# Holding one constants transfer behind the activation-table load, and moving a second norm tile to ScalarE, in a fused spectral-mixer kernel

## Chip, cores, metric

One core of a Trainium2 chip. The metric is device time in microseconds (us) of one execution.

## The reference, cut to what matters

```python
def reference(A_x, A_w_r, A_w_i, B_x, B_w1, B_b1, B_w2, B_b2):
    x = A_x                                               # (1, 2048, 512) bf16
    h = x + _A_ref(_layernorm(x, axis=-1), A_w_r, A_w_i)  # rfft2 -> times (w_r + i w_i) -> irfft2
    h2 = h + _B_ref(_layernorm(h, axis=-1), B_w1, B_b1, B_w2, B_b2)  # layernorm, MLP along the sequence, gelu
    return h2
```

The kernel does the transforms as matmuls with constant DFT matrices. Taking off a row's mean changes only the zero frequency along the row, which becomes zero and is left out of the transform, so the first stage needs only the row's reciprocal deviation, and that is multiplied into the DFT constants (not into x).

## The kernel before

x lies in 16 tiles of 128 rows x 512. For each tile: statistics of x, a reciprocal root (`rs`), the scaling of that tile's constants FP into FS (`fs`), then four matmuls of FS with x (`f1`), then an evacuation (`ys`), which copies the result out of TensorE's accumulators to Y. All of Y is needed before the second stage (`f2`). The order of this front is given by hand, engine by engine:

```python
STAT_ACT = (3,)                      # tiles whose statistics ScalarE makes; VectorE makes the others
FS_ENG = {0: "act", 3: "act", 7: "act", 9: "dve", 11: "dve", ...}   # who scales the constants; the rest GpSimd
FRONT = {
    "dve": """bn_0 ag_0 bn_1 ag_1 bn_2 bn_4 ag_2 bn_5 ag_4 bn_6 ag_5 bn_7 ag_6 bn_8 ag_7 bn_9 ag_8 ...
    "act": """rs_0 fs_0 rs_1 s1_3 s2_3 rs_2 rs_3 fs_3 rs_4 ys_0 rs_5 ys_1 ys_3 rs_6 ...
    "pool": """fs_1 bv_3 fs_2 fs_4 fs_5 fs_6 fs_8 fs_10 fs_12""",
    ...
}
WARM_AFTER = (3, 2, 0, 1, 1, 0, 0, 1, 0, 0, 0, 0, 0, 0, 0, 0)  # matmuls on zeros behind the n-th tile of f1
# ... (cut)
for q, (a, b) in enumerate(((0, 2), (2, 4), (4, 6), (6, 8), (8, 12))):
    ldx(a, b, 99 - q)                # x by tiles, SyncE's queue
ldf(2, 90)                           # constants piece 2 (tiles 8-11)
ldx(12, 16, 89)
ldf(3, 88)
ldf(0, 92, "act")                    # piece 0 (tiles 0-3), 256 KB, ScalarE's queue
ldf(1, 91, "act")                    # piece 1 (tiles 4-7), 256 KB, ScalarE's queue
act("table", T["tb"][:, 0:1], EPS[:, 0:1], ACT.Abs_reciprocal_sqrt, 1, ...)   # loads the table
# ... (cut)
def stat_act(i):                     # two passes over the tile on ScalarE, sums by accumulator
    act(f"s1_{i}", junk()[:, :], x, ACT.Identity, 512, ins=[x], accum=SM[:, i:i + 1], prio=25)
    act(f"s2_{i}", junk()[:, :], x, ACT.Square, 512, ins=[x], accum=V1[:, i:i + 1], prio=25)
    # ... bv_i on GpSimd, then rs_i on ScalarE, then fs_i
# bn_i / ag_i: bn_stats and bn_aggr of tile i on VectorE, then rs_i on ScalarE, then fs_i
```

Each engine runs its list strictly in order and waits on counters of the others: an instruction whose input is late holds up everything behind it in its list. The whole kernel:

## Time and profile before

| | before |
|---|---|
| time, median of 3 runs | 131.98 us (131.97 to 132.01) |
| span of the profiled run | 130.2 us |
| TensorE busy | 93% of the span |
| VectorE / ScalarE / GpSimd busy | 54% / 48% / 8% |
| second stage starts (end of the front) | 18.09 us |
| x 0-1, 2-3, 6-7, 8-11 landed | 4.64, 6.13, 7.38, 8.85 us |

A tile's landing is read as the issue's start plus its time to landing.

### The profile page before, as it was taken

What the parts mean: (1) busy time and instruction counts of PE and PEld (TensorE: products, weight loads), DVE (VectorE), ACT (ScalarE), POOL (GpSimd) and SP (SyncE); (2) the same over time, 40 slices, a digit from 0 to 9 for tenths busy, and PEclk for the clock granted to TensorE, in tenths of its full rate; (3) what the DMA queues carried; (4) which work ended last, traced back from release to release, by engine and by line L of the source; (5) the groups of instructions that cost most, each with busy time, mean ns of one, the idle gap of its engine ahead of it and who ended that gap; (6) DMA issues with size and microseconds to landing.
All of it is one profiled execution on the core that took longest, in us unless ns stands there. A gap on an engine that the chain in (4) does not pass through costs nothing.

```text
span 130.2 us, 1995 instructions
## 1 busy us (share of the span) xinstructions
PE 121.6 (93%) x763; PEld 73.6 (57%) x773; DVE 70.2 (54%) x130; ACT 62.8 (48%) x144; POOL 10.7 (8%) x30
## 2 busy tenths in 40 slices
PE   6799889999978989999999999999999999999990
PEld 2155656788766645544444444456666666666660
DVE  0599868999973999999981000000332422423322
ACT  4299975969866999957679622222000000000000
POOL 0089910000300000000000000000000000000000
PEclk9999999999999999999999999999999999999999
DMA  3999999999999999995000000000112112111121
GB/s 98 353 401 377 286 276 289 294 241 264 369 425 423 408 409 409 417 267 151 0 0 0 0 0 0 0 5 0 40 40 81 40 40 81 45 62 59 40 81 43
DMA packets 17337, 22.17 MB, mean 170 GB/s; under 512 B 2768, under 2 KB 13264, under 8 KB 17328
## 3 DMA queue, kind: packets, MB, share of 16 engines
q1 hardware_dynamic: 17040, 21.52, 49.1%
q10 hardware_dynamic: 288, 0.52, 1.2%
q8 instruction: 6, 0.10, 0.3%
q14 instruction: 3, 0.02, 0.1%
HBM read 19.95 MB, written 2.10 MB: 169 GB/s over the span
## 4 chain that ended last, share of the span: by engine, by line
PE 76%; ACT 12%; DVE 6%; DMA 3%; issue 2%
PE ps L556 75%; ACT Y L574 4%; DVE V L826 3%; DMA X<-in_A_x_dram 3%; ACT rs L574 2%; ACT JK L574 2%; ACT EO L574 2%; ACT FS L574 1%; DVE Y L743 1%; ACT PQ L574 1%; DVE OUT L931 1%; DVE st L681 1%; DVE FS L659 0%; PE ps L647 0%; ACT r L574 0%
## 5 line engine op out<-in xcount | busy, mean ns | idle before, releaser
L556 PE MATMUL ps<-HH,W 128*128 128x512 bf16 (+1 forms) x173 | 40.1, 380 | 0.4 <-DVE TT L894 0.2
L556 PE MATMUL ps<-GT,W 128*128 128x512 bf16 (+1 forms) x172 | 37.9, 379 | 0.2
L931 DVE SCALAR_TENSOR_TENSOR OUT<-ps,B2f,H 128x512 bf16<-128x512 f32 x16 | 12.0, 751 | 46.8 <-PE ps L556 46.8
L556 PEld LDWEIGHTS ps<-GT,W 128*128 128x128 bf16 (+1 forms) x176 | 25.5, 145 | 12.6
L556 PEld LDWEIGHTS ps<-HH,W 128*128 128x128 bf16 (+1 forms) x176 | 17.4, 100 | 19.4 <-issue 0.6
L826 DVE TENSOR_TENSOR V<-ps,W 128x2048 bf16<-128x2048 f32 (+1 forms) x8 | 15.8, 2020 | 0.3
L574 ACT ACTIVATE JK<-H,nm 128x512 bf16<-128x512 bf16 x16 | 11.6, 723 | 3.9 <-DVE H L901 3.7
L574 ACT ACTIVATE GT<-ps,B1f 128x512 bf16<-128x512 f32 (+1 forms) x11 | 7.0, 691 | 12.8 <-PE ps L556 12.7
L681 DVE BATCH_NORM_STATS2 st<-X 128x6 f32<-128x512 bf16 x15 | 9.8, 666 | 3.6 <-DMA X<-in_A_x_dram 3.6
L901 DVE TENSOR_TENSOR H<-ps,TT 128x512 bf16<-128x512 f32 x16 | 10.9, 683 | 0.1
L574 ACT ACTIVATE PQ<-ps 128x512 bf16<-128x512 f32 (+1 forms) x16 | 9.2, 588 | 3.6 <-PE ps L556 3.5
L556 PE MATMUL ps<-EM,V 128*128 128x128 bf16 x128 | 9.8, 220 | 0.4 <-ACT PQ L574 0.3
L556 PE MATMUL ps<-FS,X 128*128 128x256 bf16 x64 | 8.6, 274 | 1.1 <-ACT FS L574 0.5
L574 ACT ACTIVATE EO<-ps 128x512 bf16<-128x512 f32 x16 | 9.2, 594 | 0.9 <-PE ps L556 0.9
L574 ACT ACTIVATE CS<-ps 128x512 bf16<-128x512 f32 (+1 forms) x16 | 8.9, 588 | 1.2 <-PE ps L556 1.2
L556 PEld LDWEIGHTS ps<-EM,V 128*128 128x128 bf16 x128 | 7.9, 98 | 2.3 <-issue 1.1
L556 PE MATMUL ps<-EM,Y 128*128 128x256 bf16 x64 | 8.8, 273 | 0.4 <-DVE Y L743 0.4
L556 PE MATMUL ps<-EM,PQ 128*128 128x256 bf16 x64 | 8.6, 273 | 0.5 <-ACT PQ L574 0.5
L647 PE MATMUL ps<-ZT 128*128 128x512 bf16 x19 | 7.0, 487 | 2.3 <-DVE ZT L594 1.2
L574 ACT ACTIVATE Y<-ps 128x512 bf16<-128x512 f32 (+1 forms) x15 | 7.9, 566 | 0.2
L892 DVE TENSOR_TENSOR TT<-ps,X 128x256 f32<-128x256 f32 x16 | 6.7, 419 | 2.4 <-PE ps L556 2.4
L659 POOL TENSOR_SCALAR FS<-FP,rs 128x256 bf16<-128x256 bf16 x8 | 7.4, 938 | 6.6 <-ACT rs L574 6.4
(38 smaller groups left out, 76.9 us busy)
## 6 DMA issues: line engine op xcount, KB each, us to landing
W<-in_B_w_dram SPq DMA_DIRECT2D x8, 688.0 KB, 9.5
W<-in_B_w_dram SPq DMA_DIRECT2D x10, 512.0 KB, 16.3
out_dram<-OUT SPq DMA_DIRECT2D x16, 128.0 KB, 1.7
W<-in_A_w_r_dram SPq DMA_DIRECT2D x4, 257.0 KB, 4.5
W<-in_A_w_i_dram SPq DMA_DIRECT2D x4, 257.0 KB, 5.4
X<-in_A_x_dram SPq DMA_DIRECT2D x4, 256.0 KB, 5.1
X<-in_A_x_dram SPq DMA_DIRECT2D x2, 512.0 KB, 6.7
W<-in_A_w_r_dram SPq DMA_DIRECT2D x4, 192.8 KB, 3.5
```

Of the source, the lines that this page charges most:

```text
L556: return K.op(name, "pe", lambda eng, bank: eng.matmul(outf(bank), lhsT, rhs, start=start, stop=stop), ins=ins or [lhsT, rhs], occ=occ, la ...
L574: return eng.activation(dst, s, func, **kw)
L647: return K.op(name, "pe", lambda eng, bank: eng.matmul(ps[:, bank, :], ZT[:, 0:NP], ZT[:, :], start=True, stop=True), ins=[ZT[:, :]], occ= ...
L659: dve(f"fs_{i}", lambda eng, bank: eng.tensor_scalar(FS[:, i, :, :], FP[:, i, :, :], rs, None, op0=ALU.mult), [FP[:, i, :, :], rs], [FS[:, ...
L681: dve(f"bn_{i}", lambda eng, bank, i=i, x=x: eng.bn_stats(ST[:, i, 0:6], x), [x], [ST[:, i, 0:6]], 512, prio=25)
L743: dve(name, lambda eng, bank: eng.tensor_copy(dst, src(bank)), [], [dst], n, unit=unit, prio=28, last=last)
L826: return eng.tensor_tensor(vout, s, win, ALU.mult)
L892: dve(f"tl_{s2}", lambda eng, bank, tt=tt, xl=xl: eng.tensor_tensor(tt[:, 0, :], ps[:, bank, 256:512], xl, ALU.add), [xl], [tt[:, 0, :]], ...
L901: return eng.tensor_tensor(hs.rearrange("p (h d) -> p h d", h=2), e, tt[:, :, :], ALU.add)
L931: dve(f"fin{s2}", lambda eng, bank, dst=dst, bia=bia, hs=hs: eng.scalar_tensor_tensor(dst, ps[:, bank, :], bia, hs, op0=ALU.add, op1=ALU.add),
```

## The change

The intent: keep piece 1 of the constants, which only tile 4 and later need, out of the way of the first x tiles; use ScalarE's idle time before the first root for a second tile's statistics; adapt the order of the front to that. Core of the diff:

```diff
-STAT_ACT = (3,)
+STAT_ACT = (1, 3)
-FS_ENG = {0: "act", 3: "act", 7: "act", 9: "dve", ...}
+FS_ENG = {3: "act", 7: "act", 5: "dve", 9: "dve", ...}
 FRONT = {
-    "dve": """bn_0 ag_0 bn_1 ag_1 bn_2 bn_4 ag_2 bn_5 ag_4 bn_6 ag_5 bn_7 ag_6 bn_8 ag_7 bn_9 ag_8 ...
+    "dve": """bn_0 ag_0 bn_2 ag_2 bn_4 bn_5 ag_4 bn_6 ag_5 bn_7 ag_6 bn_8 ag_7 fs_5 bn_9 ag_8 ...
-    "act": """rs_0 fs_0 rs_1 s1_3 s2_3 rs_2 rs_3 fs_3 rs_4 ys_0 rs_5 ys_1 ys_3 rs_6 ...
+    "act": """s1_1 s2_1 rs_0 rs_1 rs_2 s1_3 s2_3 rs_4 rs_3 fs_3 ys_0 rs_5 ys_1 rs_6 ys_3 ...
-    "pool": """fs_1 bv_3 fs_2 fs_4 fs_5 fs_6 ...
+    "pool": """bv_1 fs_0 bv_3 fs_1 fs_2 fs_4 fs_6 ...
-N_GATED = 2
-WARM_AFTER = (3, 2, 0, 1, 1, 0, 0, 1, 0, 0, 0, 0, 0, 0, 0, 0)
+GATED = (("bn_0", 2), ("s2_1", 2))
+WARM_AFTER = (3, 0, 0, 0, 0, 1, 0, 0, 1, 0, 0, 0, 3, 0, 0, 0)
-LAST_WARM = 7
+LAST_WARM = 12
-    ldf(1, 91, "act")
-    act("table", ...)
+    table = act("table", ...)
+    ldf(1, 91, "act", after=[table])
```

The warm-ups (matmuls on zeros, meant to keep TensorE's clock from falling) are regrouped too: two more run early, and three now stand behind tile 12's matmuls (the rest of the diff is cut).

More of the change, by code (lines that the diff above doesn't have):

```diff
@@ L492, in memory_layout @@
     return L
-STAT_ACT = (3,)
-RS_GROUPS = ((0,), (1,), (2,), (4,), (5,), (6, 7), (8,), (9, 10), (11, 12), (13,), (14, 15))
-FS_ENG = {0: "act", 3: "act", 7: "act", 9: "dve", 11: "dve", 13: "dve", 14: "dve", 15: "dve"}
+STAT_ACT = (1, 3)
+RS_GROUPS = ((0,), (2,), (4,), (5,), (6, 7), (8,), (9, 10), (11, 12), (13,), (14, 15))
+FS_ENG = {3: "act", 7: "act", 5: "dve", 9: "dve", 11: "dve", 13: "dve", 14: "dve", 15: "dve"}
 Y_EVAC = (("single", ("act",), ("act",)),) * 6 + (("single", ("dve",), ("act",)), ("single", ("dve",), ("act", "act")))
 FRONT = {
-    "dve": """bn_0 ag_0 bn_1 ag_1 bn_2 bn_4 ag_2 bn_5 ag_4 bn_6 ag_5 bn_7 ag_6 bn_8 ag_7 bn_9 ag_8 bn_10 ag_9 bn_11 ag_10 bn_12 ag_11
+    "dve": """bn_0 ag_0 bn_2 ag_2 bn_4 bn_5 ag_4 bn_6 ag_5 bn_7 ag_6 bn_8 ag_7 fs_5 bn_9 ag_8 bn_10 ag_9 bn_11 ag_10 bn_12 ag_11
         fs_9 ag_12 bn_13 fs_11 ag_13 bn_14 bn_15 ag_14 ag_15 fs_13 fs_14 fs_15 ys_12 ys_14
         tl_0 th_0 h_0 tl_1 th_1 h_1 hh_0""",
-    "act": """rs_0 fs_0 rs_1 s1_3 s2_3 rs_2 rs_3 fs_3 rs_4 ys_0 rs_5 ys_1 ys_3 rs_6 ys_2 fs_7 rs_8 ys_4 ys_5 rs_9 ys_7 rs_11 ys_6 ys_8
-        rs_13 ys_9 ys_10 rs_14 ys_11 ys_13 yh_150 yh_151
+    "act": """s1_1 s2_1 rs_0 rs_1 rs_2 s1_3 s2_3 rs_4 rs_3 fs_3 ys_0 rs_5 ys_1 rs_6 ys_3 ys_2 rs_8 fs_7 ys_5 rs_9 ys_4 ys_6 rs_11 ys_7 ys_8
+        ys_9 rs_13 ys_10 rs_14 ys_11 ys_13 yh_150 yh_151
         eo_0 eo_1 eo_2 eo_3 eo_4 q_0 r2_0 eo_5""",
-    "pool": """fs_1 bv_3 fs_2 fs_4 fs_5 fs_6 fs_8 fs_10 fs_12""",
-    "pe": """f1_0 f1_1 f1_3 f1_2 f1_4 f1_5 f1_7 f1_6 f1_8 f1_9 f1_10 f1_11 f1_12 f1_13 f1_14 f1_15""",
+    "pool": """bv_1 fs_0 bv_3 fs_1 fs_2 fs_4 fs_6 fs_8 fs_10 fs_12""",
+    "pe": """f1_0 f1_1 f1_3 f1_2 f1_5 f1_4 f1_6 f1_7 f1_8 f1_9 f1_10 f1_11 f1_12 f1_13 f1_14 f1_15""",
 }
 N_WARM = 9
-N_GATED = 2
-WARM_AFTER = (3, 2, 0, 1, 1, 0, 0, 1, 0, 0, 0, 0, 0, 0, 0, 0)
+GATED = (("bn_0", 2), ("s2_1", 2))
+WARM_AFTER = (3, 0, 0, 0, 0, 1, 0, 0, 1, 0, 0, 0, 3, 0, 0, 0)
 V_SPLIT = (7,)
-LAST_WARM = 7
+LAST_WARM = 12
 MM1B_FROM = {5: 54000.0, 6: 62000.0}
@@ L600, in build_kernel @@
     ldf(0, 92, "act")
-    ldf(1, 91, "act")
-    act("table", T["tb"][:, 0:1], EPS[:, 0:1], ACT.Abs_reciprocal_sqrt, 1, ins=[EPS[:, 0:1]], prio=95)
+    table = act("table", T["tb"][:, 0:1], EPS[:, 0:1], ACT.Abs_reciprocal_sqrt, 1, ins=[EPS[:, 0:1]], prio=95)
+    ldf(1, 91, "act", after=[table])
     dma("ld_EMR", EM[:, 0:2048], cin["EMR"][:, :], 1 << 19, outs=[EM[:, 0:2048]], prio=44)
@@ L695, in build_kernel @@
             stat_dve(g)
-    bn0 = [o for o in K.ops if o.name == "bn_0"]
-    for w_ in range(N_GATED):
-        warm(f"warmb{w_}", wu, 50, after=bn0, occ=427.0)
+    for g_, n_ in GATED:
+        for w_ in range(n_):
+            warm(f"warm_{g_}_{w_}", wu, 50, after=[o for o in K.ops if o.name == g_], occ=427.0)
     f1u, lastmm = {}, {}
```

## The prediction

> **What bounds the kernel now.** I read four views in this order: the chain that ended last, the timeline of each engine in the first 20 us, the transfers of the first 5 us, and the timeline of VectorE between 18 and 40 us.
>
> The chain in order of time shows where an earlier front could pay.
>
> ```profile
> 0.72 3.92 DMA X<-in_A_x_dram
> 4.67 0.71 DVE st L681
> 5.39 0.20 DVE mv L682
> 5.61 0.30 ACT rs L574
> 5.94 0.51 ACT FS L574
> ...
> 6.70 1.23 ACT JK L574 x4
> ...
> 16.26 0.48 DVE FS L659 x2
> 16.74 1.21 DVE Y L743 x2
> 17.95 0.14 issue
> 18.09 13.40 PE ps L556 x163
> 31.48 0.02 issue
> 31.51 4.50 DVE V L826 x2
> ```
>
> Start, length, what. Nothing runs for 4.64 us but the arrival of the first two x tiles; then one statistics pair on VectorE, and from 5.61 to about 16.2 us ScalarE with hardly a break (the windows give it 5.00 busy in 10 to 15 us, 4.32 in 5 to 10). The second DFT stage starts at 18.09 us, when all of Y is evacuated. After 46 us the chain is matmuls to the end at 127 us, so what the front gains is handed on only if everything between 18 and 46 us moves too.
>
> The start of ScalarE's work, from its timeline (start, length, instruction, idle before):
>
> ```profile
> 5.61 0.29 ACT L574 ACTIVATE rs<-mv,eps 128x1 f32<-128x1 f32 x1 [3.01 <-DVE mv L682]
> 5.94 0.51 ACT L574 ACTIVATE FS<-FP,rs 128x256 bf16<-128x256 bf16 x1
> 6.41 0.29 ACT L574 ACTIVATE rs<-mv,eps 128x1 f32<-128x1 f32 x1
> 6.61 0.61 ACT L574 ACTIVATE JK<-X 128x512 bf16<-128x512 bf16 x1
> ```
>
> ScalarE idles 3.01 us before 5.61, 0.94 us of it with x already there. That is the hole which tile 1's statistics are to fill.
>
> The transfers in half-microsecond stretches (last three columns: granted clock, DMA share, GB/s):
>
> ```profile
> 2.00:2.50 0.50, 0.50 (x3) 0.22 (x2) 0.00 (x0) 0.49 (x2) 0.00 (x0) 1.00 0.46 147
> 2.50:3.00 0.50, 0.50 (x3) 0.23 (x2) 0.00 (x0) 0.10 (x1) 0.00 (x0) 1.00 0.87 270
> 3.00:3.50 0.50, 0.50 (x3) 0.16 (x2) 0.00 (x0) 0.00 (x0) 0.00 (x0) 1.00 0.81 287
> 3.50:4.00 0.50, 0.50 (x2) 0.15 (x1) 0.00 (x0) 0.00 (x0) 0.00 (x0) 1.00 0.95 324
> ```
>
> The engines are near saturation from 2.5 us. The landing times in the trace: constants piece 0 at 4.46 us, x 0-1 at 4.64, constants piece 1 at 5.66, x 2-3 at 6.13, x 4-5 at 6.77, x 6-7 at 7.38. The packet records by queue put some 160 KB of piece 1 in front of x's 4.64.
>
> VectorE from 18 us:
>
> ```profile
> 19.91 2.36 DVE L811 TENSOR_TENSOR V<-ps,W 128x1024 bf16<-128x1024 f32 x2 [0.76 <-PE ps L556]
> 22.41 15.98 DVE L826 TENSOR_TENSOR V<-ps,W 128x2048 bf16<-128x2048 f32 x8
> ```
>
> The filter products run back to back, about 2.28 us each, and end at 38.39. The fourth of the big ones starts at 29.16 us and is the first to need the last group of filter weights, whose final transfer (issued at 22.34, 6.3 us to landing) is down at 28.67. VectorE's wait for that passed at 28.71, so the weights have only about 0.45 us to spare.
>
> **What the Trainium skill says.** "DMA: Bandwidth & Descriptors", section "Issuing engines are not separate DMA queues": transfers issued by ScalarE and SyncE end up on the same 16 engines and interleave; its section "Queues, rings and completion order" says that each engine takes turns between queues packet by packet. The trace agrees: until 3.75 us the two queues move near-equal amounts, and x's 256 KB takes 3.92 us from issue to landing. "ScalarE: Activation LUTs", section "What ACT_TABLE_LOAD costs", gives about 1.28 us for the load itself; this trace has 1.28 (1.10 to 2.38), then the dummy activation 2.40 to 2.60, so a transfer held for that is issued near 2.65 instead of 1.17. "TensorE: Matmul & The Clock Gate", section "The HAM clock gate", says that an idle TensorE falls to half its clock over windows of about 3.4 us; here the first nine warm-up matmuls start 0.43 us apart and the later ones 0.22 us apart, which agrees, and the granted clock reads 1.00 throughout, so that column does not tell the two apart.
>
> **The change, part by part.**
>
> *Piece 1 held.* 512 KB of piece 0 and x 0-1 would then share the engines alone. The windows sum to 0.5 x (147+270+287+324) = 514 KB by 4.0 us, with some 40 KB before 2.0; so both are through at about 3.9, and landed by 4.1 to 4.2 (estimate; last packet to landing was 0.3 us for x 0-1). Gain for x 0-1: about 0.5 us. But piece 1's first packet comes about 1 us after its issue (issue 0.71, first packet 1.70 for piece 0), at 3.7, just as piece 0 ends. It then shares with x 2-3. The four transfers together are the same 1 MB as before, so x 2-3 lands between 5.7 and 6.1 (6.13 before), and x 4-5 and everything later as before. The lead of 0.5 us melts within one transfer.
>
> *Tile 1's statistics to ScalarE.* VectorE loses one statistics pair, 0.66 to 0.85 us, and takes the scaling of tile 5, 0.28 (0.20 from start to start). ScalarE gains two passes, 1.22 us (6.61 to 7.83 for tile 3's), loses the scaling of tile 0, 0.47 from start to start, and both reciprocal roots stay. Net +0.75 us on the engine that bounds the front; but it starts at about 4.2 in place of 5.61, 1.4 us earlier. Were there no other wait, ScalarE would be 0.65 us ahead.
>
> *The wait that eats it.* In the new order ScalarE runs the statistics of tiles 1, two roots, and then rs_2 before s1_3. rs_2 needs the statistics of tile 2, which need x 2-3: landing about 5.95, statistics 0.71, aggregate 0.20, rs_2 at about 6.86. Then 0.19 to s1_3, 1.22 for its two passes, rs_4 0.19, rs_3 0.33 to the dependent scaling, scaling 0.40: the first evacuation at 6.86+0.19+1.22+0.19+0.33+0.40 = 9.19 us, against 9.04 before. With x 2-3 at 5.6 it would be 8.85. So ScalarE comes out between 0.2 ahead and 0.15 behind there.
>
> *From there to the second stage.* Eleven evacuations at 0.475, six roots at 0.19 and one scaling at 0.40 make 6.77 us to rs_14: 15.96 or earlier, against 15.91, where 0.09 was a wait for the statistics of tile 12. VectorE, with one tile less, is 0.1 to 0.5 us ahead by then, and the order puts rs_9 one evacuation earlier, which removes its 0.31 us idle before the scaling of tile 9. The two short waits near the end (0.14 before the evacuation of tile 13, 0.26 before that of tile 15) may shrink as well. I take 0.2 us for the front, with 0.2 us either way.
>
> *Tile 0 on GpSimd.* Its scaling costs 0.93 there against 0.51, so the first real matmul comes at about 6.65 against 6.50: no bound, as ScalarE's first evacuation is at 9. GpSimd has seven scalings from tile 2 on before, six after; it falls from bound to not bound.
>
> *Warm-ups.* Two more of them, in TensorE's idle time: nothing, if the clock stays up. TensorE will be idle for about 1.2 us between the warm-ups after tile 0 and tile 1's matmuls.
>
> *Behind 18 us.* The front's gain is handed on one to one until the lead meets the 0.45 us of the filter weights. Their landing does not move: the issuing order of SyncE stays and the total in front of them too. So a gain above about 0.4 us is cut off there.
>
> Sum: 131.98 - 0.2 = 131.78 us.
>
> **Rivals.** (a) x 2-3 also lands early, say at 5.5, because held-back piece 1 comes last: ScalarE then gains 0.4 to 0.6 us in the front, and the filter weights cut it to 0.4: 131.5. For it: the intent, and that ScalarE's order was adapted to it. Against: the packet turns. (b) ScalarE really is 0.15 us or more behind after the stop at rs_2, and nothing is recovered: 132.1. For it: ScalarE is at 5.00 of 5.00 between 10 and 15 us and has net more work. Against: the waits at the end of the front. (c) TensorE's clock drops in the thinner stretch around 8 to 9 us: f2 at half rate for about 3.4 us would cost up to 1.5 us: 133. Against: idles of 0.5 us in today's front do no harm, and warm-ups follow tiles 5, 8 and 12. (d) A changed interleaving of stages after 18 us, as the build schedules by its own model: 0.2 us either way.
>
> **Range and chances.** 2% is 2.64 us; the whole stretch that the change can touch, from 4.6 to 18.1 us, could hardly lose a fifth, and no rival gives more than 1.5 us. The run-to-run spread is 0.04 us. From (a) with some margin to (b): 131.4 to 132.15. Within 2%: 0.98.
>
> **What would show it.** Right: the first statistics at 4.1 to 4.3 us; x 2-3 at 5.7 to 6.1; ScalarE idle between the roots of tiles 0 and 1 and that of tile 2; the second stage starting at 17.7 to 18.1; a start of the fourth big filter product not before 28.7. Wrong: x 0-1 still near 4.6 (then no gain); x 2-3 by 5.5 and no idle of ScalarE (rival a); warm-ups or tile matmuls at double spacing after 6 us (rival c); a shift before 18 us that isn't found again at 46 us for a reason other than the filter weights.

## The result, and the profile after

132.22 us median (131.99 to 132.32, 4 runs) against 131.97 (131.94 to 132.01). The ratio is 1.0016, 95% interval 0.9998 to 1.0033. (A ratio is the mean time of one kernel's fast runs over that of the other's of the same rounds, so not quite the ratio of the medians.) By the 2% measure it is "same", as predicted; but 132.22 lies outside the stated range, on the slow side, and a gain of 0.2 us had been forecast. A later repeat gave 132.02 (ratio 1.0001, 0.9989 to 1.0013), inside the range, and still no gain. Single runs scatter more than the 0.04 us that the prediction went by: the changed kernel's over 0.33 and 0.40 us in the two timings, the kernel before's over 0.46 to 1.22 us in the three batches of eleven runs below. So which side of 132.15 the median falls on is partly chance; that there is no gain of 0.2 us is not.

The chain that ended last, after the change (start, length, what):

```profile
1.63 4.82 DMA X<-in_A_x_dram
...
6.48 1.29 DVE st L681 x2
...
8.90 0.49 ACT Y L574
...
9.41 0.92 POOL FS L659
...
10.64 0.94 POOL FS L659
...
11.62 0.61 PE ps L556 x4
...
15.71 0.82 PE ps L647 x3
16.53 0.89 PE ps L556 x8
...
17.44 0.70 DVE Y L743
...
18.28 13.40 PE ps L556 x163
...
31.70 4.50 DVE V L826 x2
```

Before, ScalarE carried the front to 16.2 us. Now the chain runs through x 4-5, ScalarE, GpSimd and then TensorE's own queue, and three of its matmuls at 15.71 come from line 647: warm-ups on zeros. GpSimd's scaling at 10.64 is tile 6's, and its timeline has it wait for the root of tiles 6 and 7:

```profile
10.64 0.93 POOL L659 TENSOR_SCALAR FS<-FP,rs 128x256 bf16<-128x256 bf16 x1 [0.30 <-ACT rs L574]
```

From the matmuls that it releases at 11.62, TensorE's queue runs to 17.41 without a wait of 0.2 us. Two single warm-ups, at 12.23 and 13.44, lie in that stretch too; without the three late ones TensorE waits 0.28 us at tile 13 (shown below), so there they do not bind. The second stage starts at 18.28 us, 0.19 later than before, and that is found again everywhere behind: the fifth big filter product at 31.70 in place of 31.51, the end of the span at 130.4 in place of 130.2. All of the difference was made before 18.3 us.

The end of the front, from TensorE's timeline before:

```profile
16.07 1.58 PE L556 MATMUL ps<-FS,X 128*128 128x256 bf16 x12 [0.22 <-DVE FS L659]
18.09 0.38 PE L556 MATMUL ps<-EM,Y 128*128 128x256 bf16 x2 [0.44 <-DVE Y L743]
```

and the same stretch of the changed kernel's timeline, with VectorE's scalings and the last root between:

```profile
15.67 0.28 DVE L659 TENSOR_SCALAR FS<-FP,rs 128x256 bf16<-128x256 bf16 x1
...
15.71 0.82 PE L647 MATMUL ps<-ZT 128*128 128x512 bf16 x3
15.89 0.34 ACT L574 ACTIVATE rs<-mv,eps 128x2 f32<-128x2 f32 x1
...
16.27 0.49 DVE L659 TENSOR_SCALAR FS<-FP,rs 128x256 bf16<-128x256 bf16 x2 [0.33 <-ACT rs L574]
16.36 1.47 PE L556 MATMUL ps<-FS,X 128*128 128x256 bf16 x12
```

Before, tile 13's matmuls start at 16.07, 0.06 us after its scaling ended. Now that scaling ends at 15.95, but the matmuls stand behind the warm-ups and start at 16.36. The last root (of tiles 14 and 15) is at 15.89 against 15.91: up to there the front is neither faster nor slower.

How ScalarE's lead was lost by then: its first evacuation in the kernel before,

```profile
9.04 0.57 ACT L574 ACTIVATE Y<-ps 128x512 bf16<-128x512 f32 x1
```

and its timeline after the change:

```profile
8.81 0.58 ACT L574 ACTIVATE Y<-ps 128x512 bf16<-128x512 f32 x1
...
9.47 0.58 ACT L574 ACTIVATE Y<-ps 128x512 bf16<-128x512 f32 x1
10.25 0.30 ACT L574 ACTIVATE rs<-mv,eps 128x2 f32<-128x2 f32 x1 [0.20 <-DVE mv L682]
```

The first evacuation came at 8.81, 0.23 us earlier than before. Then the root of tiles 6 and 7 waits for VectorE's aggregate of tile 7; an evacuation takes 0.47 from start to start, so that root could have started at 9.95, and 0.30 us are lost.

The transfers explain VectorE's lateness: it stood waiting for x twice (its timeline has 0.19 us before tile 4's statistics and 0.28 before tile 6's, with no wait there before the change). The second of these:

```profile
8.12 0.69 DVE L681 BATCH_NORM_STATS2 st<-X 128x6 f32<-128x512 bf16 x1 [0.28 <-DMA X<-in_A_x_dram]
```

From the windows view, the stretch 5.5 to 7 us (columns as in the prediction: at the end the granted clock, DMA share and GB/s) of the kernel before:

```profile
5.50:7.00 1.50, 1.02 (x6) 0.34 (x6) 1.47 (x5) 1.35 (x4) 0.20 (x1) 1.00 1.07 414
```

and of the changed kernel:

```profile
5.50:7.00 1.50, 1.22 (x4) 0.24 (x2) 1.27 (x3) 1.39 (x6) 1.02 (x2) 1.00 0.94 315
```

| landed at, us | before | after |
|---|---|---|
| x 0-1 | 4.64 | 4.48 |
| x 2-3 | 6.13 | 5.35 |
| x 4-5 | 6.77 | 6.45 |
| x 6-7 | 7.38 | 8.10 |
| x 8-11 | 8.85 | 9.40 |
| constants piece 1 | 5.66 | 8.74 |

The first six tiles of x come earlier, the next six later, and the amount moved per us is lower while the held piece is under way.

### The profile page after: what moved, and what is told of

It reads as the page before. It is cut to its first block, busy times and chain, and to the rows that moved or that the text cites. A ratio compares the mean times of both kernels' runs of the same rounds, so it can differ in the third digit from the quotient of the medians.

```text
span 130.4 us, 2013 instructions
## 1 busy us (share of the span) xinstructions
PE 123.3 (95%) x775; PEld 73.8 (57%) x775; DVE 70.3 (54%) x129; ACT 63.6 (49%) x147; POOL 11.1 (9%) x31
## 4 chain that ended last, share of the span: by engine, by line
PE 80%; DVE 6%; ACT 5%; DMA 4%; issue 1%; POOL 1%; SPq 1%; POOLq 0%
PE ps L556 79%; DMA X<-in_A_x_dram 4%; DVE V L826 3%; ACT EO L574 2%; PE ps L647 2%; POOL FS L659 1%; ACT JK L574 1%; DVE st L681 1%; ACT PQ L574 1%; SPq L546 1%; DVE OUT L931 1%; DVE Y L743 1%; ACT FS L574 0%; ACT Y L574 0%; ACT rs L574 0%
## 5 line engine op out<-in xcount | busy, mean ns | idle before, releaser
L681 DVE BATCH_NORM_STATS2 st<-X 128x6 f32<-128x512 bf16 x14 | 9.2, 673 | 3.9 <-DMA X<-in_A_x_dram 3.9
L647 PE MATMUL ps<-ZT 128*128 128x512 bf16 x23 | 8.5, 502 | 1.6 <-DVE ZT L594 1.2
L556 PEld LDWEIGHTS ps<-FS,X 128*128 128x128 bf16 x64 | 5.7, 98 | 3.9 <-POOL FS L659 2.1
```

What stands on the lines that cost most here:

```text
L556: return K.op(name, "pe", lambda eng, bank: eng.matmul(outf(bank), lhsT, rhs, start=start, stop=stop), ins=ins or [lhsT, rhs], occ=occ, la ...
L647: return K.op(name, "pe", lambda eng, bank: eng.matmul(ps[:, bank, :], ZT[:, 0:NP], ZT[:, :], start=True, stop=True), ins=[ZT[:, :]], occ= ...
L681: dve(f"bn_{i}", lambda eng, bank, i=i, x=x: eng.bn_stats(ST[:, i, 0:6], x), [x], [ST[:, i, 0:6]], 512, prio=25)
```

## The experiments

The theory after reading the traces was: (1) the three warm-ups behind tile 12 delay the last three tiles' matmuls; (2) the hold, by making x 6-11 late, costs more than it gains. Rivals: the warm-ups are needed for the clock; the hold is what helps, and moving tile 1 is what hurts. Twelve runs were made (eleven edited kernels, and the changed kernel once more), all correct, each timed in five rounds against the kernel before on the same chip; each four rows of the table share a chip. The second column is that kernel's median in that batch.

| kernel | us | before, us | ratio (95%) | second stage starts, us |
|---|---|---|---|---|
| changed, no late warm-ups | 131.81 | 131.96 | 0.9979 (0.9964 to 0.9993) | 18.35 |
| before, with late warm-ups | 132.64 | 131.96 | 1.0046 (1.0032 to 1.0060) | 18.52 |
| changed, not held | 132.60 | 131.96 | 1.0042 (1.0030 to 1.0054) | 18.66 |
| changed, not held, no late warm-ups | 132.35 | 131.96 | 1.0040 (1.0012 to 1.0067) | 18.30 |
| changed, repeat | 132.02 | 131.93 | 1.0001 (0.9989 to 1.0013) | 18.26 |
| changed, held longer, no late warm-ups | 136.02 | 131.93 | 1.0318 (1.0293 to 1.0342) | 22.16 |
| changed, piece 1 in x's queue, no late warm-ups | 132.00 | 131.93 | 0.9998 (0.9982 to 1.0014) | 18.12 |
| before, held | 131.74 | 131.93 | 0.9982 (0.9970 to 0.9994) | 17.91 |
| tile 7 aggregated first, no late warm-ups | 131.73 | 132.09 | 0.9971 (0.9945 to 0.9997) | 18.02 |
| tile 7 aggregated first, late warm-ups | 131.99 | 132.09 | 0.9985 (0.9960 to 1.0009) | 18.06 |
| x 8-11 in halves, no late warm-ups | 132.00 | 132.09 | 1.0006 (0.9970 to 1.0042) | 18.14 |
| both of these, no late warm-ups | 132.15 | 132.09 | 1.0001 (0.9976 to 1.0027) | 18.38 |

The last column is of the one profiled run, which was not always typical: that of the first row took 132.28 us, the slowest of its six, with x 4-5 landing at 6.97.

**The late warm-ups.** Taken out of the changed kernel, and put alone into the kernel before:

```diff
-WARM_AFTER = (3, 0, 0, 0, 0, 1, 0, 0, 1, 0, 0, 0, 3, 0, 0, 0)
-LAST_WARM = 12
+WARM_AFTER = (3, 0, 0, 0, 0, 1, 0, 0, 1, 0, 0, 0, 0, 0, 0, 0)   # after_no_tail
+LAST_WARM = 8
```

```diff
-WARM_AFTER = (3, 2, 0, 1, 1, 0, 0, 1, 0, 0, 0, 0, 0, 0, 0, 0)
-LAST_WARM = 7
+WARM_AFTER = (3, 2, 0, 1, 1, 0, 0, 1, 0, 0, 0, 0, 3, 0, 0, 0)   # before_tail
+LAST_WARM = 12
```

> The changed kernel without the three warm-up matmuls behind tile 12. Theory 1 (those warm-ups stand in TensorE's queue in front of tile 13's matmuls at the end of the front): tile 13 starts near 15.98 us when its scaling is ready, in place of 16.36, the second stage starts at 18.0 to 18.1 in place of 18.28, and the time falls by 0.2 to 0.3 us to 131.95 to 132.05. Theory 2 (the late x 6-7 alone made the loss): no change, 132.2. Theory 3 (the warm-ups hold up the clock): matmuls of the second stage start 0.21 us apart in place of 0.11, and the time rises by 0.5 us or more.

> The kernel before with three warm-ups added behind tile 12's matmuls, nothing else. Theory 1: tile 13's matmuls come 0.2 to 0.4 us later than their 16.07, the second stage starts at 18.3 to 18.45, and the time rises by 0.2 to 0.35 us to 132.2 to 132.3. Theory 2: no change, 131.97.

Without them 131.81, 0.41 below the changed kernel's first timing and 0.21 below its repeat (which was on another chip); with them in the old kernel 132.64, 0.68 above it on the same chip. TensorE's timeline of the old kernel with warm-ups:

```profile
15.95 0.82 PE L647 MATMUL ps<-ZT 128*128 128x512 bf16 x3
16.61 1.47 PE L556 MATMUL ps<-FS,X 128*128 128x256 bf16 x12
```

and of the changed kernel without:

```profile
16.18 1.73 PE L556 MATMUL ps<-FS,X 128*128 128x256 bf16 x12 [0.28 <-DVE FS L659]
```

The first pair shows tile 13 going from 16.07 to 16.61, the second tile 13 waiting for its scaling again and for nothing else. Theory 1 holds. A yardstick free of the scatter in x's arrival is the time from the end of the last VectorE scaling to the start of the second stage: 1.35 us in the kernel before, 1.74 with warm-ups; in the changed kernel 1.51 with and 1.35 without. So they cost about 0.39 in the old kernel and 0.16 in the new, where tile 12's matmuls come 0.24 us earlier (15.04 against 15.28) and so push less. The medians say more than that: 0.68 in the old kernel, and 0.25 and 0.26 for the two pairs of the new order that share a chip (below). The profiled run of the old kernel with warm-ups was the fastest of its six (132.40), so part of the 0.68 is not in its trace, and what it is isn't shown. Theory 3, that they hold up the clock, falls: without them the second stage's matmuls still start 0.11 us apart.

**The hold undone.**

```diff
     ldf(0, 92, "act")
+    ldf(1, 91, "act")                    # after_unheld; after_unheld_no_tail: and no late warm-ups
     table = act("table", ...)
-    ldf(1, 91, "act", after=[table])
```

> The changed kernel with piece 1 of the constants issued at once again, nothing else. Theory 2 (holding delays x 6-7 and loses throughput): x 6-7 lands near 7.4 us in place of 8.10, x 0-1 at about 4.64 in place of 4.48, the root of tiles 6 and 7 (10.25 in the changed kernel) comes 0.2 to 0.4 us earlier; with the warm-ups still at the end the time falls by 0.1 to 0.3 us. Theory 1 alone: the warm-ups follow tile 12, so at most 0.1 us is gained. If x first was really worth something, the time rises by 0.1 to 0.2 us.

> Both undone: piece 1 at once and no warm-ups behind tile 12; the two norm tiles on ScalarE and the new order stay. If both theories hold and add: second stage at 17.8 to 17.95, time 131.7 to 131.85, below both kernels. If only the warm-ups matter: the same as the changed kernel without them, about 132.0.

Theory 2 falls, with its sign reversed: without the hold the time rises to 132.60, and without late warm-ups to 132.35 against 131.81 with the hold on the same chip, 0.54 us worse. The traces show x 6-7 back at 7.50 and 7.31 as expected, x 8-11 at 8.95 and 8.69; what I had weighed wrongly is x 2-3, at 6.20 and 6.00 in place of 5.35. ScalarE's timeline of the changed kernel without the hold:

```profile
7.16 0.30 ACT L574 ACTIVATE rs<-mv,eps 128x1 f32<-128x1 f32 x1 [0.81 <-DVE mv L682]
```

This is the root of tile 2, which stands before tile 3's statistics in the new list. It is 0.84 us later than with the hold (6.32), and ScalarE idles 0.81 us for it. So the new order leans on the hold: two norm tiles on ScalarE in the new order, without the hold and without late warm-ups, are 0.39 us slower than the kernel before (132.35 against 131.96). No run moves tile 1 alone, so what part of this is tile 1's and what part the order's is not shown. The warm-ups' cost shows here too: 0.25 us between these two.

**The repeat.** The same kernel, unedited.

> The changed kernel once more, on the same chip as the next three. Theory: 132.1 to 132.3 us, and the second stage starts 1.5 us after the end of the last scaling on VectorE, as in its first profile, because of the warm-ups behind tile 12. If it comes out at 131.8, the loss in the first timing was chance of the chip and the warm-ups cost nothing.

132.02, a little below what I expected and above the 131.8 that would have cleared the warm-ups. Second stage less last scaling is 1.52 us.

**The hold alone.** In the kernel before:

```diff
-    ldf(1, 91, "act")
-    act("table", ...)
+    table = act("table", ...)
+    ldf(1, 91, "act", after=[table])
```

> The kernel before with piece 1 of the constants held and nothing else: no norm tile moved, no order changed. If holding is worth 0.4 to 0.5 us by itself: 131.5. By the traces, tile 0's statistics start 0.05 to 0.2 us earlier and nothing else waits for x in the old order until x 6-7, so I expect 0.1 to 0.2 us, 131.8; if x 6-7 comes at 8.1 as in the changed kernel it is needed at 8.0 there and takes 0.1 back.

131.74, at the good end of what I expected from the traces, and the steadiest of the faster kernels (131.66 to 131.83 in five runs). ScalarE's timeline, first instruction:

```profile
5.43 0.29 ACT L574 ACTIVATE rs<-mv,eps 128x1 f32<-128x1 f32 x1 [2.82 <-DVE mv L682]
```

x 0-1 landed at 4.46, the root is at 5.43 in place of 5.61, and the second stage at 17.91 in place of 18.09: 0.18 us, handed through unchanged. x 6-7 was late here as well (8.14) and cost nothing visible, as its statistics are due at 8.23.

**Held longer.** ScalarE issues piece 1 behind the root of tile 2 (a dependency added in the program):

```diff
+    held = next(o for o in K.ops if o.name == "rs_2")
+    fp1.deps.append((held, True)); held.consumers.append(fp1)      # fp1 = ldf(1, 91, "act")
```

> The changed kernel without the late warm-ups, and with piece 1 held still longer: ScalarE issues it at about 6.6 us, while the first statistics pass of tile 3 runs. Theory (the held piece is what makes x 6-7 late, and x 6-7 is what takes ScalarE's lead back at the root of tiles 6 and 7): x 6-7 lands at 7.0 to 7.4 us in place of 7.9 to 8.1, no idle of ScalarE before the root of tiles 6 and 7, time 131.4 to 131.6. Rival (the throughput is lost whenever a second queue starts, whatever it carries): x 6-7 as late as before, 131.8. Risk: piece 1 lands after 9.4 us and holds up the scaling of tile 4.

x 6-7 did land early, at 6.72. But piece 1, issued at 6.7, took 6.6 us and landed at 13.25 (VectorE's timeline: the scaling of tile 5):

```profile
13.35 0.31 DVE L659 TENSOR_SCALAR FS<-FP,rs 128x256 bf16<-128x256 bf16 x1 [3.07 <-DMA FP<-c_FP]
```

136.02 us: the risk named beforehand came true, larger than I thought. The packet records by queue have no packet of it before 10.47 us, 3.8 us after the issue: it was not moved slowly all that time, it began late. In the changed kernel, too, its first packet is at 4.74 us, 2.1 us after the issue at 2.63. This run also shows the clock that my rival (c) feared, from the windows view of this kernel:

```profile
13.00:14.00 1.00, 0.28 (x3) 0.26 (x4) 0.65 (x2) 0.00 (x0) 0.59 (x1) 1.00 1.11 320
...
15.00:16.00 1.00, 0.94 (x5) 0.21 (x3) 1.00 (x4) 0.86 (x4) 1.00 (x2) 0.50 1.17 292
```

After 3.60 us of TensorE idle, the granted clock (third from the end) falls from 1.00 to 0.50 and is back at 1.00 from 18 us. The idle stretches of the changed kernel's TensorE after its first matmul are 0.48 us or less and leave it at 1.00.

**Piece 1 in x's own queue**, behind x 6-7:

```diff
     ldf(0, 92, "act")
+    ldf(1, 95.5)                         # SyncE's queue, between x 6-7 and x 8-11
-    ldf(1, 91, "act", after=[table])
```

> The changed kernel without the late warm-ups, piece 1 put into the queue of x itself, behind x 6-7: no second queue after piece 0. Theory: x 2-3 by 5.3, x 4-5 by 6.1, x 6-7 by 6.9 us; time 131.4 to 131.6. Against it: SyncE issues one transfer of 0.5 us more ahead of the filter weights, so their last group may land near 29.1 in place of 28.7 and cut the gain at the fourth big filter product.

x 2-3 at 5.38, x 4-5 at 6.08, x 6-7 at 7.12, near what was expected, but 132.00 us. VectorE now waits one tile later:

```profile
9.45 0.69 DVE L681 BATCH_NORM_STATS2 st<-X 128x6 f32<-128x512 bf16 x1 [0.57 <-DMA X<-in_A_x_dram]
```

That is tile 8: x 8-11 landed at 9.43, as late as with the held second queue, and the root of tiles 6 and 7, whose aggregate stands behind tile 8's statistics, is at 10.26 again. The windows view has 313 GB/s from 5.5 to 7 us here too. So x 6-7 was not the only late piece, and a second queue is not what lowers the rate. The filter weights landed later as feared, at 29.28, and the fourth big product started at 29.31; by the fifth that was made up (13.42 us after the start of the second stage, as in the kernel before).

**Tile 7 aggregated first**, so that ScalarE's root no longer waits for x 8-11; with and without the late warm-ups:

```diff
-    bn_7 ag_6 bn_8 ag_7 fs_5
+    bn_7 ag_6 ag_7 bn_8 fs_5             # ag7_tail; ag7_no_tail: and no late warm-ups
```

> The changed kernel without the late warm-ups, and VectorE aggregates tile 7 before the statistics of tile 8 instead of after them. Theory 4 (ScalarE's lead is lost at the root of tiles 6 and 7, which waits for tile 7's aggregate, which stands in VectorE's queue behind tile 8's statistics, which wait for x 8-11 at 9.2 to 9.4 us): that root comes straight after the evacuation before it, about 9.95 in place of 10.23 to 10.46, and ScalarE's lead lasts to the root of tiles 14 and 15 (15.6 to 15.7); time 131.5 to 131.65 against 131.8. Rival (VectorE itself, late by x 8-11, binds at the end): the early root gains nothing, 131.8.

> The same order with the three warm-ups behind tile 12 left in. Theory 1: slower than the same kernel without them, on the same chip, by 0.2 to 0.4 us; second stage 1.5 us after the end of the last VectorE scaling, against 1.35 without. Rival: no difference.

131.73 without, 131.99 with: the warm-ups cost 0.26 us once more (1.51 us against 1.35 on the yardstick). ScalarE, in the kernel without them, runs through:

```profile
9.65 0.58 ACT L574 ACTIVATE Y<-ps 128x512 bf16<-128x512 f32 x1
10.13 0.29 ACT L574 ACTIVATE rs<-mv,eps 128x2 f32<-128x2 f32 x1
```

The wait is gone, as theory 4 says, but the kernel is hardly faster than 131.81 (ratios 0.9971 and 0.9979 with overlapping intervals). In this profiled run x 0-1 landed only at 4.89, so ScalarE had no lead to lose. The run with the late warm-ups compares better with the changed kernel: its first evacuation is at the same place (8.80 against 8.81), and its last root at 15.70 in place of 15.89, the second stage at 18.06 in place of 18.28. So in the trace the lead now lasts. That removing this wait gains time in the medians is not shown, as the changed kernel itself was not timed on this chip.

**x 8-11 in halves**, alone and with the order above:

```diff
-    ((0, 2), (2, 4), (4, 6), (6, 8), (8, 12))
+    ((0, 2), (2, 4), (4, 6), (6, 8), (8, 10), (10, 12))
```

> The changed kernel without the late warm-ups and x 8-11 fetched in two halves, so that tile 8 waits for 256 KB and not for 512. Theory 4: x 8-9 lands at 8.6 to 8.8, tile 8's statistics no longer wait (before 8.9 to 9.1 where x 6-7 is not late), the root of tiles 6 and 7 comes at about 10.0; time 131.5 to 131.7. Rival (x 6-7 at 8.0 already sets tile 8's time): no change, 131.8.

> Both: tile 7 aggregated before tile 8's statistics, and x 8-11 in halves. If theory 4 holds and VectorE is no bound, 131.4 to 131.6, below both kernels of this study; the filter weights' last group (28.6 to 28.9 us) cuts any gain at the start of the fourth big filter product, so not below 131.4.

132.00 and 132.15: misses. x 8-9 did land at 8.49 and 8.74, and tile 8 no longer waited. But the last group of filter weights landed at 29.45 and 29.92 in place of 28.67. SyncE has one transfer more to issue here, which may be the cause but isn't shown to be: without any such transfer, the kernel not held and without late warm-ups had them at 29.33. VectorE's timeline of the second kernel, fourth big filter product:

```profile
29.94 2.29 DVE L826 TENSOR_TENSOR V<-ps,W 128x2048 bf16<-128x2048 f32 x1 [0.40 <-PE ps L556]
```

It starts 0.02 us after the weights' landing, 0.40 us idle. The profile names TensorE there; the instruction waits for two things, and the landing shows which was the last. The fifth product then comes 13.77 us after the start of the second stage (13.54 in the first kernel), against 13.42 before: 0.35 and 0.12 us lost to the weights. The cut that the prediction drew at 28.7 us is real in kind: this product cannot start before the weights are there. No front here was early enough to meet it at 28.7. In the same kernel, with the wait at the root of tiles 6 and 7 gone, the next root waits 0.46 us for VectorE's aggregate of tile 8: the wait moved one place on, as the rival said.

## Why the prediction was wrong, step by step

- **Warm-ups ("nothing, if the clock stays up"): wrong, and the step that pushed the result out of the range.** I counted them as work in idle time and did not ask where in the queue they stand. Three of them stand in front of tile 13's matmuls, whose scaling is ready 0.4 us before they are done. They cost 0.16 us on the yardstick in the changed kernel and 0.2 to 0.4 in times (0.25 and 0.26 where a pair shares a chip). The kernel without them takes 131.81, against the 131.78 of my sum, though the agreement is partly chance, as the next points say.
- **The front ("I take 0.2 us"): wrong in size.** Up to the last root the profiled run gained 0.02 us (15.89 against 15.91). The lead of 0.23 at the first evacuation was there, better than the 0.15 behind to 0.2 ahead that I gave; the wait at the root of tiles 6 and 7 took 0.30 back. The prediction's own sum for ScalarE gave no gain here (15.96 or earlier against 15.91): the 0.2 rested on the two short waits near the end, which were to shrink. With 0.475 us an evacuation they come to 0.40 together before, to 0.63 after, and to 0.51 without the late warm-ups.
- **x 0-1 0.5 us earlier: wrong.** It was 0.16 (4.48), and 4.41 to 4.89 in the other kernels with the hold, against 4.63 to 4.68 in those without. SyncE's queue had started 256 KB by 3.78 us (4.04 before), as the sum of bytes said; but the landing came 0.70 us after that (0.60 before), where I had allowed 0.2 to 0.3. Why is not shown.
- **"The lead of 0.5 us melts within one transfer", x 2-3 between 5.7 and 6.1: wrong.** It landed at 5.35. I let piece 1 share evenly with x 2-3 from 3.7 us on, 1 us after its issue. Its first packet came at 4.74, and from 4.5 to 5.5 us ScalarE's queue moved 18 KB and SyncE's 330. So the landing of rival (a) came true, but not its gain of 0.4 to 0.6 us: the next waits took it.
- **"x 4-5 and everything later as before": wrong.** x 6-7 came 0.72 later and x 8-11 0.55. Every kernel with piece 1 held or moved moved 247 to 356 GB/s from 5.5 to 7 us; the four with it issued at once, 406 to 419.
- **The stop at the root of tile 2: right as a mechanism.** ScalarE idles before it, 0.12 us with the hold and 0.81 without. With that root at the measured 6.32 the sum gives 8.65 for the first evacuation; it was 8.81, as the root of tile 4 came about 0.14 us late behind VectorE's wait for x 4-5.
- **Net cost of tile 1 on ScalarE: not tested alone.** Without the hold and the late warm-ups, the two norm tiles and the new order together lose 0.39 us.
- **Handed on one to one until the filter weights: right.** 0.19 at 18.3 us is 0.19 at 31.7; the kernel before with the hold shows the same for a gain (0.18 at both places); the split kernels show late weights binding.
- **Clock: right.** The granted clock stayed at 1.00. The idle of about 1.2 us forecast before tile 1's matmuls did not come: tile 0 was late, and the warm-ups behind it run on to tile 1's start at 8.58.
- **GpSimd ("falls from bound to not bound"): wrong.** Tile 0's matmuls came at 7.11 us (6.65 forecast) and bound nothing. But GpSimd, which no piece of the chain names before, is in the chain of both profiles of the changed kernel: tile 6's scaling at 10.64, late by the root of tiles 6 and 7, releases the stretch of TensorE's queue that ends in the late warm-ups.
- **Rival (b)'s 132.1 is near the result by luck.** It had ScalarE behind at the first evacuation; ScalarE was 0.23 us ahead.

In sum: predicted -0.20 + 0 (warm-ups); measured in the profile -0.02 up to the last root, +0.04 from that root to the end of the last scaling (0.87 in place of 0.83), and +0.17 from there to the second stage. That is the 0.19.

Open: why the transfers run slower between 5.5 and 8 us when piece 1 is not issued at once (278 to 367 GB/s against 401 to 416). It is not the second queue (piece 1 in x's queue does it too) and not piece 1's bytes being ahead (held longer, its first packet came after x 8-11, which still landed only at 9.48). Nor is it shown how much of the scatter between runs of the changed kernel comes from this.

Two versions beat the kernel before by a little, in one batch each (their intervals end at 0.9993 to 0.9997): the kernel before with the hold alone (131.74, steady), and the changed kernel without late warm-ups (131.81, or 131.73 with tile 7 aggregated first). What the rest of the change adds to the hold is too small to be seen here.

## What to carry to other kernels

A filler instruction on an in-order queue is free only if the next real instruction isn't ready before the filler ends; look for that one instruction, not for the engine's idle share. Holding back a transfer that isn't needed yet can pay by itself, but check each later landing, as what is held comes back among them and, behind other transfers, can begin far later than its issue suggests. Try each part of a combined change alone: here one line gave as much as the best versions of the whole change.

## What the Trainium skill lacked or had wrong

- "DMA: Bandwidth & Descriptors", section "Queues, rings and completion order", says that engines take turns between queues packet by packet. From 5.5 to 6.5 us the two queues moved 128 and 172 KB, which does not contradict it. It does not say how late a transfer's first packet can come behind another queue's transfers: 1.0 us after the issue for piece 0, 2.1 for the held piece 1, 3.8 when that was issued at 6.7 us. The held piece took 6.1 and 6.6 us to land, against 4.5 when issued at 1.17 us. Whether its packets waited for turns or were not there yet, the records do not tell.
- No page has it: from 5.5 to 7 us the queues together moved 406 to 419 GB/s with piece 1 issued at once, and 247 to 356 with it held or moved.
- "TensorE: Matmul & The Clock Gate", section "The HAM clock gate", agrees where it was tested: after 3.60 us idle the granted clock was 0.50 from about 14.3 to 17.7 us (worked out from readings of 0.65 in 14 to 15 us and in 17 to 18), some 3.4 us, with TensorE busy again from 13.72. It warns that clock events in traces can be unreliable, but does not say that the profile's clock column reads 1.00 during the cold start, when matmuls start 0.43 us apart.
